# Window attention and a gated feed-forward layer on one core: the whole order of the work written anew, with 363 operations on other engines

## Chip, cores and metric

One of the eight cores of a Trainium2 chip runs one program. The metric is device time in microseconds (us), of which less is better: the median of three runs. A profiled execution of the same program gives the rows below.

## What is computed

```python
# q, k, v: 8 batches x 8 heads x 576 tokens x 64, float32
scores = q @ k.T / sqrt(64)
mask   = (0 <= i - j) & (i - j < 64)              # causal window of 64 tokens
attn   = softmax(where(mask, scores, -1e9))
x      = (attn @ v)                               # as 4608 tokens x 512
h      = x @ w_in                                 # 512 x 2048
g      = h * erf(softplus(h))
out    = g @ w_out                                # 2048 x 512
```

## The kernel before

The 4608 tokens are 36 **units** u of 128 tokens, two units make a **chunk** c of 256, and each chunk has two **groups** g (g = 2c and 2c + 1), one for each half of the 2048 hidden columns. Every float32 operand is split into two float16 parts, high and low, and a product is the sum of three float16 products.

What each instruction does is in some sixty small functions (handlers) at the lines 374 to 805. In which order they are issued is in one string, PLAN, at the lines 52 to 245: 2,696 tokens such as `E:16:0:v`, each a handler's name, its numbers, and often the engine (v VectorE, a ScalarE, g GpSimd). The loop that reads it is the kernel's last:

```python
with tc.manual_schedule(engines=CORE | {ET.SP}):
    for tok in PLAN.split():
        name, *args = tok.split(":")
        HANDLERS[name](*(int(a) if a.isdigit() else a for a in args))
```

Each engine carries out its own instructions in the order of the tokens, and so does SyncE's queue with the DMAs; an instruction waits on semaphores for what it needs. So PLAN decides two things: behind which work on its engine an operation stands, and on which engine it runs.

The stations of the work, by the tokens that this text names:

- **Loads** (SyncE): `lq lk lv` a unit's q, k, v (520 KB for v); `L` one of 16 loads of 1 MB of weights. Weights are split into their parts early (`c d o b h l`, lines 586 to 644).
- **Attention** of unit u: `s` scores (TensorE, line 437), `m` mask and row maximum (VectorE, 454), `f` subtract it (460), `e` two exponentials of a half unit (ScalarE, 474), `r` the low part (482), `t` a transpose by DMA (486), `a` times v (TensorE, 489), `n` normalize (500).
- **Input of the layer**: `xh xl xt`, `T yh yl yt` (529 to 564) split x, form sums of its blocks (`T`, line 545) and turn them by DMA.
- **First matrix product** for groups from 8 on: seven products `M:g:1` to `M:g:7` (line 737; 24 matmuls of 128 columns each) of block sums, after Strassen's scheme. Products 1, 6, 7, 4 are added up in PSUM bank 0, products 2 and 5, 3 in bank 1. Between them `E:g:0` to `E:g:3` (take, line 754) copy bank 0 out, and `C:g:0` to `C:g:2` (join, line 757) add bank 1 to what was copied. The next product into a bank has to wait for the copy before it.
- **Gate**: `sp` softplus and `er` erf (ScalarE, 764 and 768), `gt` (VectorE, 771), `gh gl` the two parts of the result (775, 782).
- **Second matrix product**: `mA` 8 matmuls and `mB` 4 matmuls of 512 columns (line 786), two of each per half group and output bank. `fo` (result, line 795) scales one of the two output banks `o` into `ob`; only then may the next chunk's `mA` write into that bank. `st` stores.

```python
def take(g, k, eng):                                                   # E
    narrow(eng, corner(g, *((0, 0), (0, 1), (1, 1), (1, 0))[k]), bank_view(0))
def result(g, j, eng="v"):                                             # fo
    c, hf = ORDER[g]
    o, co, dst = ops[j], st_g[g], ob[c % 2 if c < 2 else 0][:, j, :]
    if hf == 0 or joint(g):
        scaled(eng, dst, o, co)
```

`e`, `sp` and `er` each need a function table of ScalarE that the other two don't use; where the order goes from one to another, a table load stands ahead. Copies and scalings on ScalarE need none. `narrow` and `scaled` are the helpers at lines 513 and 363, so a row of `E` on ScalarE stands at L515, on VectorE at L517, one of `fo` at L365 or L367; `C` stands at L759, `M` at L745, `mA` and `mB` at L791.

In PLAN the tokens of the last four chunks repeat from chunk to chunk almost word for word; those ahead of them repeat nowhere.

Of the kernel before, what the change touches and what calls it, by code (L numbers as in the profile page):

```python
# [19 lines left out]
W = 64  # L20
# [32 lines left out]
    "lq:0 lv:0 lk:0 lm L:0 lv:1 s:0 pk:0:2:v c:0 m:0:1 m:0:0 f:0:1:g L:1 lq:1 f:0:0:v pk:1:2:v tp:0:1 d:0 e:0:1 pa:0 "  # L53
    "o:0 tp:0:0 pb:0 e:0:0 px:0 d:1 c:1 o:1 py:0 lk:1 L:8 b:0:a pc:0 b:1:a L:3 s:1 a:0:0 L:9 m:1:1 L:2 c:8 d:8 m:1:0 "
    "f:1:0:g lq:2 a:0:1 mb:0 lk:2 o:8 mx:0 my:0 mc:0 c:3 h:0:a n:0 h:1:a d:3 f:1:1:g tp:1:0 e:1:0 tp:1:1 c:9 d:9 "
    "e:1:1 xp:0 c:2 xh:0:a l:0 L:11 o:3 s:2 o:9 d:2 o:2 m:2:1 f:2:1:g b:8:a m:2:0 b:3:a L:10 a:1:0 xl:0 c:11 a:1:1 "
    "b:9:a tp:2:1 b:2:a f:2:0:g tp:2:0 n:1 mb:1 e:2:1 l:1 lq:3 xp:1 d:11 lk:3 lv:2 c:10 xh:1:a L:4 mx:1 e:2:0 o:11 "
    "b:11:a lq:4 lv:3 my:1 mm:0:0:0 d:10 s:3 mc:1 lk:4 xl:1 mb:4 h:3:a a:2:1 c:4 o:10 d:4 l:3 m:3:1 o:4 m:3:0 "
    "pk:3:2:v mm:0:0:1 mm:0:1:1 a:2:0 h:2:a f:3:1:g pk:2:2:v pk:4:0:a L:5 mm:0:1:0 b:10:a b:4:a tp:3:1 mx:4 my:4 "
    "lk:5 pa:1 pb:1 f:3:0:g lq:5 l:2 px:1 c:5 d:5 py:1 L:7 mb:5 pk:5:1:a e:3:1 pc:1 dc:0:g ev:0:1:a d:7 n:2 ev:0:0:a "  # L60
    "o:5 L:6 lv:4 c:7 tp:3:0 pk:4:1:a e:3:0 U:0:7:0:0:g pk:5:0:a xh:2:a a:3:1 a:3:0 U:0:7:1:0:v o:7 pk:4:2:v "
    "mm:0:2:1 mc:4 mm:0:2:0 d:6 mm:0:3:0 n:3 mx:5 my:5 W:0 b:5:a mc:5 mb:2 lv:5 pk:5:2:v U:0:7:2:0:g pa:2 mx:2 c:6 "
    "xl:2:g xh:3:v pb:2 xt:3:0 xl:3:v b:7:a ev:0:2:a sp:0:0 h:8:a px:2 xt:3:1 h:9:g my:2 mm:0:3:1 py:2 er:0:0 h:10:a "
    "xt:2:0 V:0 l:8 o:6 pc:2 mm:1:0:1 qh:5:v mc:2 ev:0:3:a xt:2:1 mm:1:1:1 kh:5:a gt:0:0 b:6:a l:10 l:9 dc:1:g mb:3 "
    "h:4:a mm:1:1:0 mm:1:0:0 qh:4:v vh:5:a kh:4:g h:5:a ev:1:1:a kl:4 ql:4 mm:1:3:1 h:11:a kl:5 ev:1:0:a l:5 lk:7 "
    "sp:0:1 mm:1:3:0 mm:1:2:0 s:4 l:4 l:11 ql:5 vl:5 lq:6 L:12 mm:1:2:1 gh:0:0:a Uh:0:7:0:a m:4:0 vh:4:a mA:0:0:1 "
    "mx:3 gn:0:v mA:0:0:0 m:4:1 vl:4 my:3 ev:1:3:v sp:1:0 er:0:1 ev:1:2:a mc:3 h:6:v Ul:0:7:0:g er:1:0 s:5 gt:0:1 "
    "L:13 mm:2:0 h:7:a dc:2:v c:12 d:12 mm:2:1 gl:0:0 o:12 lv:7 c:13 lk:6 pk:7:1:a mB:0:0:0 l:7 d:13 pk:6:0:a "
    "pk:6:1:a ev:2:0:a mB:0:0:1 lv:6 l:6 f:4:0:g gh:0:1:a o:13 e:4:0 mm:2:2 ev:2:1:a U:1:7:0:0:v f:4:1:g lq:7 "
    "pk:7:0:a mA:0:1:1 gl:0:1 pk:7:2:v pk:6:2:v pa:3 U:1:7:1:0:v pb:3 r:4:0:g e:4:1 px:3 mm:2:3 m:5:0 f:5:0:v py:3 "  # L70
    "r:4:1:v U:1:7:2:0:g pc:3 b:13:a b:12:a m:5:1 t:4:0 qh:7:g dc:4:g t:4:1 mA:0:1:0 mb:6 mB:0:1:1 e:5:0 gt:1:0 mx:6 "
    "f:5:1:v my:6 ev:2:3:v ev:2:2:a mm:3:0 mc:6 kh:6:a e:5:1 h:13:v a:4:0 r:5:1:v dc:3:v a:4:1 gh:1:0:v mB:0:1:0 "
    "ql:7 h:12:a mm:3:1 n:4 r:5:0:g ev:3:0:a sp:2:0 t:5:0 l:12 fo:0:1:a mm:3:2 vh:6:g lq:9 fo:0:0:a l:13 t:5:1 "
    "sp:1:1 kh:7:a L:14 a:5:0 L:15 a:5:1 kl:6 qh:6:v ql:6 vl:6 s:6 ev:3:1:a kl:7 mm:3:3 m:6:1 sp:2:1 vh:7:g d:14 "
    "er:1:1 er:2:0 xh:4:a f:6:1:g n:5 e:6:1 xh:5:a gl:1:0 mA:1:0:1 mB:1:0:1 m:6:0 dc:5:g lv:8 xl:4:g mA:1:0:0 gt:1:1 "
    "f:6:0:g c:15 ev:3:3:v xl:5:v d:15 xt:4:0 gh:1:1:a lq:8 c:14 lk:8 gl:1:1 e:6:0 mB:1:0:0 ev:3:2:a xt:4:1 o:14 "
# [12 lines left out]
    "xt:7:1 ev:5:3:a a:8:0 xt:7:0 e:9:0 pb:5 px:5 mm:5:2 ev:5:2:a py:5 U:1:5:0:2:v gt:4:1 U:3:7:2:0:g U:0:5:0:1:v "
    "mA:4:0:0 U:1:5:1:2:v U:0:5:1:1:v xt:6:1 mA:4:0:1 n:8 mm:6:1 pc:5 r:9:0:v dc:6:g dc:7:v e:9:1 U:0:5:2:1:v mm:6:0 "  # L90
    "gh:4:1:a vh:10:a r:9:1:v xh:8:v gt:5:0 t:9:0 qh:10:a ev:6:1:a kh:10:a gl:4:1 mm:6:3 gl:4:0 kl:10 mB:4:0:1 "
    "xt:8:0 Uh:0:5:1:a U:1:5:2:2:g t:9:1 Uh:1:5:2:a ev:6:0:a Ul:0:5:1:v ql:10 kh:11:a lq:12 ev:6:3:a Ul:1:5:2:v "
    "kl:11 vl:10 qh:11:a s:10 st:0:1 Uh:3:7:0:v a:9:1 m:10:0 ql:11 sp:5:1 a:9:0 mA:4:1:1 vh:11:g U:0:6:0:1:v st:0:0 "
    "lk:12 vl:11 m:10:1 n:9 f:10:1:v mB:4:0:0 U:1:6:0:2:v mm:7:1 sp:6:0 U:1:6:1:2:v er:5:1 s:11 mB:4:1:1 U:0:6:1:1:g "
    "gh:5:0:a lv:12 er:6:0 Uh:0:6:1:a mm:6:2 lk:13 pk:12:0:a Ul:0:6:1:v mA:5:0:1 mA:4:1:0 lv:13 mB:4:1:0 U:2:5:0:1:v "
    "f:10:0:g lq:13 Ul:3:7:0:v ev:7:1:a pk:12:1:a pk:13:0:a m:11:0 pk:13:1:a pk:13:2:v e:10:0 pk:12:2:v pa:6 gt:5:1 "
    "pb:6 gt:6:0 U:2:5:1:1:g U:2:5:2:1:g gl:5:0 Uh:1:6:2:v gh:5:1:a mA:5:0:0 Uh:2:5:1:a ev:6:2:a mB:5:0:0 e:10:1 "
    "Ul:2:5:1:v Ul:1:6:2:v mB:5:0:1 sp:6:1 r:10:0:v gh:6:0:a mm:7:0 dc:11:g m:11:1 px:6 U:3:5:0:2:v py:6 gl:5:1 "
    "U:2:6:0:1:v pc:6 ev:7:0:a U:2:6:1:1:v mm:7:3 r:10:1:g U:3:5:1:2:v f:11:1:v U:0:3:0:0:v mA:5:1:1 sp:7:0 kh:12:a "
    "U:0:3:1:0:v kh:13:a mA:5:1:0 mB:5:1:0 er:6:1 gn:5:v U:3:5:2:2:v xl:8:v kl:12 er:7:0 mB:5:1:1 kl:13 fo:5:0:a "  # L100
# [772 lines left out]
```

## Time and profile before

| | |
|---|---|
| median of 3 runs | 874.83 us (871.86 to 876.56) |
| the profiled execution, its own time | 875.01 us |
| its span in the trace | 873.2 us |
| TensorE busy | 821.2 us, 94% |
| VectorE, ScalarE, GpSimd busy | 725.9, 690.2, 230.2 us |
| mean granted TensorE clock | 0.988 |

TensorE is busy in nearly all of the span, VectorE and ScalarE in four fifths of it, though more at the beginning than at the end. A busy share alone does not say who waits for whom: that is in the waits, the timeline and the stretches.

### The profile page before, as it was taken

The numbers are of one execution on the slowest core, as the hardware profiler recorded it, in microseconds if no ns is written. First come the engines' busy times: TensorE is split into PE (matmuls) and PEld (weight loads), VectorE is DVE, ScalarE is ACT, GpSimd is POOL, SyncE is SP. The second block draws the span as 40 slices with busy tenths as digits, with TensorE's granted clock in tenths as the row PEclk, the third lists the DMA queues.
The fourth block names the chain that finished last, engine by engine and source line by source line (L and its number), as shares of the span: only waits on it lengthen the run. The fifth ranks groups of instructions, "written<-read, shape, count | busy, mean of one in ns | idle before, by whom it ended". The sixth has DMA issues, their size and how long they took to land.

```text
span 873.2 us, 25365 instructions
## 1 busy us (share of the span) xinstructions
PE 821.2 (94%) x10868; PEld 588.2 (67%) x10868; DVE 725.9 (83%) x1610; ACT 690.2 (79%) x823; POOL 230.2 (26%) x206
## 2 busy tenths in 40 slices
PE   3879999999999999998999999999999999999988
PEld 3768666576677677686666767666776767676743
DVE  5999999999999889997989798779999886545351
ACT  4999899989998988787877897477889788465541
POOL 2142352522163342233231334132102322010000
PEclk9889999999999999999999999999999999999999
DMA  9955282751584366374364736543746232220000
GB/s 357 403 169 213 49 228 60 147 153 43 86 192 114 100 166 123 98 132 123 80 143 94 143 81 128 109 109 59 168 74 167 52 74 54 45 56 2 26 25 25
DMA packets 152321, 101.92 MB, mean 117 GB/s; under 512 B 129552, under 2 KB 129680, under 8 KB 152208
## 3 DMA queue, kind: packets, MB, share of 16 engines
q1 hardware_dynamic: 152208, 100.30, 46.6%
q8 instruction: 85, 1.39, 0.7%
q14 instruction: 28, 0.23, 0.1%
HBM read 59.64 MB, written 9.44 MB: 79 GB/s over the span
## 4 chain that ended last, share of the span: by engine, by line
PE 43%; DVE 18%; ACT 10%; DMA 5%; issue 3%; SPq 1%; POOL 0%; DVEq 0%; ACTq 0%; POOLq 0%
PE o L791 22%; PE hp L745 19%; DVE y L773 2%; ACT y L765 2%; DMA pt<-p 2%; DVE vs L372 2%; DVE gl L372 2%; PE av L497 1%; DVE sm L457 1%; ACT L765 1%; DVE ks L372 1%; DVE h L759 1%; DMA vr<-v_in 1%; PE s L448 1%; DVE arena L729 1%
## 5 line engine op out<-in xcount | busy, mean ns | idle before, releaser
L791 PE MATMUL o<-w,gh 128*128 128x512 f16 x1152 | 270.2, 381 | 4.8 <-ACT ob L365 4.5
L791 PEld LDWEIGHTS <-gh 128*128 128x128 f16 x1152 | 109.3, 98 | 123.8 <-issue 7.1
L745 PEld LDWEIGHTS <-w 128*128 128x128 f16 x2688 | 157.1, 98 | 20.6 <-issue 4.0
L745 PE MATMUL hp<-arena,w 128*128 128x128 f16 x2688 | 166.3, 220 | 3.3 <-ACT h L515 1.9
L791 PE MATMUL o<-w,gl 128*128 128x512 f16 x576 | 144.5, 379 | 0.0
L745 PE MATMUL hp<-arena 128*128 128x128 f16 x2016 | 127.2, 220 | 8.2 <-DVE h L517 4.5
L745 PEld LDWEIGHTS <-arena 128*128 128x128 f16 x2016 | 118.9, 98 | 23.1 <-issue 10.7
L773 DVE TENSOR_TENSOR y<-h,y 128x1024 f32<-128x1024 f32 x72 | 90.6, 1264 | 27.2 <-ACT y L769 27.2
L765 ACT ACT_TABLE_LOAD x46 | 59.0, 1283 | 49.2 <-DVE h L759 47.2
L515 ACT ACTIVATE h<-hp 128x512 f32<-128x512 f32 x101 | 59.1, 586 | 48.5 <-PE hp L745 37.9
L701 PE MATMUL hp<-arena,w 128*128 128x256 f16 (+1 forms) x960 | 90.7, 254 | 4.7 <-DMA arena<-arena 2.2
L759 DVE TENSOR_TENSOR h<-hp,h 128x512 f32<-128x512 f32 x84 | 57.5, 685 | 43.5 <-PE hp L745 42.9
L372 DVE SCALAR_TENSOR_TENSOR gl<-y,sgc,gh 128x1024 f16<-128x1024 f32 x64 | 85.5, 1340 | 7.2 <-PE o L791 7.2
L701 PEld LDWEIGHTS <-w 128*128 128x128 f16 x960 | 78.6, 99 | 16.1 <-issue 4.4
L765 ACT ACTIVATE y<-h,c 128x1024 f32<-128x1024 f32 x72 | 81.7, 1145 | 7.6 <-DVE h L759 7.0
L791 PEld LDWEIGHTS <-gl 128*128 128x128 f16 x576 | 52.6, 98 | 50.6 <-DVE gl L372 0.2
L462 POOL TENSOR_TENSOR sm<-sm,mx 128x512 f32<-128x512 f32 x43 | 55.8, 1300 | 97.9 <-DVE mx L457 78.2
L769 ACT ACTIVATE y<-y 128x1024 f32<-128x1024 f32 x72 | 74.7, 1053 | 0.5
L484 POOL TENSOR_TENSOR p<-sm,p 128x512 f16<-128x512 f32 x31 | 43.8, 1415 | 114.7 <-ACT sm L480 105.6
L457 DVE CUSTOM_DVE_ANT_0 sm<-s,mask 128x128 f32<-128x128 f32 x288 | 65.5, 283 | 3.4 <-PE s L448 2.7
L769 ACT ACT_TABLE_LOAD x47 | 60.3, 1283 | 0.8
L480 ACT ACTIVATE sm<-sm,shift,cde 128x512 f32<-128x512 f32 x64 | 52.1, 814 | 2.1
(169 smaller groups left out, 1169.6 us busy)
## 6 DMA issues: line engine op xcount, KB each, us to landing
vr<-v_in SPq DMA_DIRECT2D x36, 520.0 KB, 4.5
kr<-k_in SPq DMA_DIRECT2D x36, 384.0 KB, 4.8
qr<-q_in SPq DMA_DIRECT2D x36, 256.0 KB, 3.7
out<-ob SPq DMA_DIRECT2D x34, 256.0 KB, 2.5
arena<-w_in SPq DMA_DIRECT2D x4, 1024.0 KB, 9.5
w<-w_in SPq DMA_DIRECT2D x4, 1024.0 KB, 9.8
arena<-w_out SPq DMA_DIRECT2D x4, 1024.0 KB, 6.6
w<-w_out SPq DMA_DIRECT2D x2, 1024.0 KB, 14.3
```

The costliest lines, as they stand in the source:

```text
L372: nc.vector.scalar_tensor_tensor(dst, src, s, hi, op0=ALU.mult, op1=ALU.subtract)
L457: nc.vector.tensor_tensor_reduce(smi(u, par)[:, j, :], sps[par][:, j, :], mask[:, var, :], 1.0, LOWEST, op0=ALU.add, op1=ALU.max, accum_ou ...
L462: eng_of(eng).tensor_tensor(s, s, m.unsqueeze(2).broadcast_to([P, HP, P]), op=ALU.subtract)
L480: nc.scalar.activation(s, s, AF.Exp, bias=shift14, scale=es)
L515: nc.scalar.activation(dst, src, AF.Copy)
L701: nc.tensor.matmul(hps[pc % 2][:, f, at_t], w1[a][hf][:, cc, fs], xt[b][c % 2][:, cc:2 * NCC:NCC, :][:, at_x, :], start=(n == 0), stop=(n ...
L745: nc.tensor.matmul(bank[:, q, f, :], left(m, a, 2 * hf + q)[:, cc, f * P:(f + 1) * P], xt[b][c % 2][:, slot + cc, :], start=m in (1, 2, 5) ...
L759: nc.vector.tensor_tensor(dst, bank_view(1), dst, op=ALU.add)
L765: nc.scalar.activation(at(yb, g, n), at(hb, g, n), AF.Softplus, scale=st_c[g][:, n:n + 1])
L769: nc.scalar.activation(y, y, AF.Erf)
L773: nc.vector.tensor_tensor(y, at(hb, g, n), y, op=ALU.mult)
L791: nc.tensor.matmul(ops[j], a[:, f // 2, j, f % 2, :], w2[b][:, hf * GF + f, :], start=f == 0 and a is gh and b == 0 and not (joint(g) and hf),
```

## The change

PLAN is another string of the same 2,696 operations; nothing else in the file differs, except that PLAN has one line more, so that every line number behind it is higher by one. Announced was "a new pattern of two units repeated from chunk 6 on, joined to the beginning; some on other engines". The string shows no such pattern: from one chunk to the next, or to the next but one, hardly half of any engine's tokens stand in the same order, in the last chunks too. The order differs from the first token on.

Of the 2,696 operations 363 run on another engine than before; most of these moves cancel. What is left, by the counts of the tokens: `fo` from 28 on ScalarE and 12 on VectorE to 19 and 21; `T` from 18 on GpSimd and 24 on VectorE to 24 and 18; `f` from 43 on GpSimd and 29 on VectorE to 46 and 26; `E` from 74 on ScalarE and 38 on VectorE to 72 and 40; `gn` from 7 on GpSimd to 12; and one to three each of `h qh kh vh xh xl yh yl pk ev gh r U Ul`. In sum ScalarE has 16 of these operations fewer (573 to 557), VectorE 5 fewer (920 to 915), GpSimd 21 more (188 to 209).

```diff
 PLAN = (
...
-    "pk:22:2:v M:16:1 gt:14:0 C:15:2 f:20:1:g lq:23 lk:23 gh:13:1:v yt:8:1:1 gt:14:1 E:16:0:v M:16:6 f:20:0:g "
...
-    "mA:33:0:0 gl:33:1 mB:33:0:1 er:34:1 M:35:4 mB:33:0:0 M:35:3 gh:34:0:v mA:33:1:1 E:35:3:v C:35:2 sp:35:0 "
-    "mA:33:1:0 gt:34:1 st:15:0 er:35:0 mB:33:1:1 gl:34:0 sp:35:1 fo:33:1:a st:16:1 mB:33:1:0 gh:34:1:v mA:34:0:1 "
...
+    "xh:18:v gt:14:1 mB:13:0:0 mA:13:1:0 pk:22:1:a gh:14:0:a st:5:1 M:15:3 pk:22:0:a M:16:1 s:21 yt:8:1:0 pk:23:2:v "
+    "pa:11 T:9:0:v e:20:1 pb:11 C:15:2 mB:13:1:1 m:21:0 f:21:0:g E:16:0:v yt:8:0:1 M:16:2 gh:14:1:a m:21:1 px:11 "
+    "fo:13:1:a mB:13:1:0 t:20:0 py:11 yt:8:1:1 pc:11 dc:18:v M:16:6 gl:14:0 mA:14:0:1 yh:9:0:a E:16:1:v xl:18:v "
...
+    "M:35:5 er:34:0 mB:33:1:0 C:35:1 M:35:4 st:15:1 M:35:3 fo:33:0:a gt:34:0 E:35:3:v gh:34:0:a gh:34:1:v gl:34:0 "
+    "st:16:0 mB:33:1:1 mA:34:0:0 C:35:2 fo:33:1:v mB:34:0:0 sp:35:0 mA:34:0:1 gl:34:1 er:35:0 mB:34:0:1 mA:34:1:0 "
...
```

ScalarE's order near the end of the program, before: from the erf of group 34 to the second erf of group 35 (h0 and y0 hold groups of even number, h1 and y1 those of odd number; hp0 is PSUM bank 0; o0 and o1 are the output banks). `L765` is softplus, `L769` erf; `ob<-o1` and `ob<-o0` are `fo:33`.

```order
L769 ACTIVATE y0_137<-y0_137 128x1024 x2
L765 ACT_TABLE_LOAD
L765 ACTIVATE y1_138<-h1_136,c1_87 128x1024
L769 ACT_TABLE_LOAD
L769 ACTIVATE y1_138<-y1_138 128x1024
L765 ACT_TABLE_LOAD
L765 ACTIVATE y1_138<-h1_136,c1_87 128x1024
L365 ACTIVATE ob_141<-o1_148,sg_88 128x512
L365 ACTIVATE ob_141<-o0_147,sg_88 128x512
L769 ACT_TABLE_LOAD
L769 ACTIVATE y1_138<-y1_138 128x1024
```

The same place in the changed order, up to the last scaling, `fo:35`:

```order
L770 ACTIVATE y0_137<-y0_137 128x1024
L366 ACTIVATE ob_141<-o0_147,sg_88 128x512
L366 ACTIVATE gh_139<-y0_137,sgc_90 128x1024
L766 ACT_TABLE_LOAD
L766 ACTIVATE y1_138<-h1_136,c1_87 128x1024
L770 ACT_TABLE_LOAD
L770 ACTIVATE y1_138<-y1_138 128x1024
L766 ACT_TABLE_LOAD
L766 ACTIVATE y1_138<-h1_136,c1_87 128x1024
L770 ACT_TABLE_LOAD
L770 ACTIVATE y1_138<-y1_138 128x1024
L366 ACTIVATE ob_141<-o1_148,sg_88 128x512
```

Before, both scalings of chunk 16's result (`fo:33`) stand behind three table loads and the first three of group 35's four softplus and erf operations. Now one of the two stands ahead of them, and the other is on VectorE.

ScalarE's order where the products of group 32 begin, before: `h0<-hp0` is `E:32:0`.

```order
L769 ACT_TABLE_LOAD
L769 ACTIVATE y0_137<-y0_137 128x1024 x2
L765 ACT_TABLE_LOAD
L765 ACTIVATE y1_138<-h1_136,c1_87 128x1024
L769 ACT_TABLE_LOAD
L769 ACTIVATE y1_138<-y1_138 128x1024
L515 ACTIVATE h0_135<-hp0_145 128x2x256
L765 ACT_TABLE_LOAD
L765 ACTIVATE y1_138<-h1_136,c1_87 128x1024
```

And in the changed order (`h1<-hp0` is `E:31:3`; `h0<-hp0` are `E:32:0`, and then `E:32:1` and `E:32:2`):

```order
L766 ACT_TABLE_LOAD
L766 ACTIVATE y0_137<-h0_135,c1_87 128x1024
L516 ACTIVATE h1_136<-hp0_145 128x2x256
L770 ACT_TABLE_LOAD
L770 ACTIVATE y0_137<-y0_137 128x1024
L516 ACTIVATE h0_135<-hp0_145 128x2x256
L366 ACTIVATE ob_141<-o0_147,sg_88 128x512
L766 ACT_TABLE_LOAD
L766 ACTIVATE y1_138<-h1_136,c1_87 128x1024
L516 ACTIVATE h0_135<-hp0_145 128x2x256 x2
```

Here three copies out of bank 0 stand each right behind an operation that loads a table, where before it was one. In the whole order ScalarE loads a table 138 times, before 129 times: for `e` 35 (32), for `sp` 49 (46), for `er` 50 (47), and 4 others.

## Rows read from the trace of the kernel before

**Rows 1.** Five stretches: busy us (instructions) by engine, clock granted, DMA share, GB/s.

```profile
0.00:100.00 100.00, 75.15 (x988) 63.02 (x989) 87.54 (x236) 83.77 (x112) 26.74 (x38) 0.93 0.68 252
100.00:275.00 175.00, 169.74 (x2136) 116.81 (x2137) 170.34 (x409) 165.72 (x208) 67.07 (x54) 1.00 0.56 130
275.00:600.00 325.00, 311.36 (x4508) 226.11 (x4504) 286.59 (x640) 260.16 (x309) 102.72 (x86) 0.99 0.51 112
600.00:825.00 225.00, 224.00 (x3001) 161.48 (x2999) 163.76 (x313) 163.41 (x179) 33.64 (x30) 1.00 0.35 73
825.00:873.20 48.20, 40.94 (x254) 20.81 (x250) 17.66 (x18) 17.10 (x17) 0.00 (x0) 0.95 0.06 23
```

**Rows 2.** TensorE timeline, the end: start, us, line, matmuls, [idle before <-releaser].

```profile
838.02 3.62 PE L791 MATMUL o<-w,gh 128*128 128x512 f16 x16
841.48 1.89 PE L791 MATMUL o<-w,gl 128*128 128x512 f16 x8
846.88 5.30 PE L791 MATMUL o<-w,gh 128*128 128x512 f16 x16 [3.51 <-ACT ob L365]
```

**Rows 3.** Timeline of ScalarE in the same stretch.

```profile
843.81 1.28 ACT L765 ACT_TABLE_LOAD   x1
845.11 1.15 ACT L765 ACTIVATE y<-h,c 128x1024 f32<-128x1024 f32 x1
846.16 1.24 ACT L365 ACTIVATE ob<-o,sg 128x512 f32<-128x512 f32 x2
```

**Rows 4.** A stretch of 5 us at the end, columns as in rows 1.

```profile
845.00:850.00 5.00, 3.12 (x11) 1.26 (x11) 0.19 (x1) 4.73 (x6) 0.00 (x0) 0.81 0.28 105
```

**Rows 5.** Waits of TensorE, whole run: us in total, times, longest us.

```profile
PE hp L745 <- ACT h L515: 5.0, 6, 2.1
PE s L469 <- POOL sm L462: 4.9, 3, 2.2
PE o L791 <- ACT ob L365: 4.5, 2, 3.5
PE hp L745 <- DVE h L517: 4.5, 2, 2.7
```

**Rows 6.** Timeline of TensorE, waits of the middle and of the last third.

```profile
396.69 1.50 PE L745 MATMUL hp<-arena,w 128*128 128x128 f16 x24
400.86 2.90 PE L745 MATMUL hp<-arena 128*128 128x128 f16 x24 [2.67 <-DVE h L517]
...
423.36 1.89 PE L791 MATMUL o<-w,gh 128*128 128x512 f16 x8 [1.01 <-ACT ob L365]
...
570.13 1.50 PE L745 MATMUL hp<-arena 128*128 128x128 f16 x24 [2.07 <-ACT h L515]
...
804.20 1.50 PE L745 MATMUL hp<-arena 128*128 128x128 f16 x24 [0.50 <-ACT h L515]
```

**Rows 7.** Timeline of ScalarE ahead of 570.13 us.

```profile
567.16 1.28 ACT L765 ACT_TABLE_LOAD   x1 [6.10 <-DVE h L759]
568.45 1.15 ACT L765 ACTIVATE y<-h,c 128x1024 f32<-128x1024 f32 x1
569.51 0.58 ACT L515 ACTIVATE h<-hp 128x512 f32<-128x512 f32 x1
```

**Rows 8.** Groups by line and shape: xcount | busy us, mean ns | idle before.

```profile
L773 DVE TENSOR_TENSOR y<-h,y 128x1024 f32<-128x1024 f32 x72 | 90.6, 1264 | 27.2 <-ACT y L769 27.2
...
L765 ACT ACT_TABLE_LOAD x46 | 59.0, 1283 | 49.2 <-DVE h L759 47.2 <-DVE den L505 1.3
...
L462 POOL TENSOR_TENSOR sm<-sm,mx 128x512 f32<-128x512 f32 x43 | 55.8, 1300 | 97.9 <-DVE mx L457 78.2 <-DVE den L505 8.2 <-DMA arena<-arena 6.0
...
L462 DVE TENSOR_TENSOR sm<-sm,mx 128x512 f32<-128x512 f32 x29 | 20.7, 720 | 0.2
...
L365 ACT ACTIVATE ob<-o,sg 128x512 f32<-128x512 f32 x26 | 17.4, 676 | 22.5 <-PE o L791 17.4 <-DMA out<-ob 5.0
...
L367 DVE TENSOR_SCALAR ob<-o,sg 128x512 f32<-128x512 f32 x8 | 5.8, 741 | 0.0
```

379 rows, old and new, of the table PLAN are left out of this document.

## Prediction, made before the changed kernel was run

> **What bounds the kernel now.** I read the stretches first, then TensorE's waits, then its timeline at the waits that matter. In the stretches [rows 1] the reader is to see where TensorE is not busy. In the first 100 us that is 100 - 75.2 = 24.8 us; there VectorE and ScalarE work 88 and 84 of 100 us, and GpSimd stands in TensorE's way too (4.9 us) [rows 5]. From 100 to 275 us it is 5.3 us, with VectorE and ScalarE busy 97% and 95%. From 275 to 600 us it is 13.6 us, though VectorE has room (287 of 325 us). From 600 to 825 us it is 1.0 us: this part, where the order repeats from chunk to chunk, is as good as TensorE allows. In the last 48.2 us it is 7.3 us. The order takes no matmul away and moves none to another engine, so the 821 us that TensorE is busy are the floor, and the change can only win or lose in these gaps, 52 us in all.
>
> Who ends the gaps of the middle stands in the waits [rows 5]: the copy of bank 0 by ScalarE (5.0 us in 6 waits) and by VectorE (4.5 us in 2), and the scaling of a result by ScalarE (4.5 us in 2, of which 3.5 us at the very end). The DMAs hardly show after the first loads.
>
> A gap can cost more than itself. After the wait of 2.67 us at 398 us, 24 matmuls take 2.90 us where the same 24 take 1.50 us elsewhere [rows 6]; after the 3.51 us at the end, 16 take 5.30 us instead of 3.62 us [rows 2], and the granted clock of that stretch is 0.81 of the 2.4 GHz level, a mean of that level and the lower one [rows 4]. So I count these two waits with 1.40 and 1.68 us on top, and give shorter ones no surcharge: after those of 1.01, 2.07 and 0.50 us the matmuls take their usual time [rows 6].
>
> **The end: -5.2 us.** Before, the two scalings of chunk 16 stand on ScalarE behind three table loads and three of group 35's operations. TensorE has the bank's last matmul done at 841.48 + 1.89 = 843.4 us [rows 2], but ScalarE begins the scaling only at 846.16 us, after the load at 843.81 us and the softplus at 845.11 us [rows 3]. The loss is 3.51 + 1.68 = 5.19 us. In the new order one scaling stands ahead of these loads and the other on VectorE, directly behind the last join; the end then hangs on group 35's chain. From the last product's end TensorE has 4 + 48 matmuls left ahead of group 35, and 16 of them take 841.48 - 838.02 = 3.46 us [rows 2], so 52 take 11.2 us. The chain before took from 838.02 to 843.81 us, 5.8 us, up to the end of the first erf [rows 2, 3]; the gate (1.26 us [rows 8]) and the high part, a VectorE operation that I put no longer than the gate, make it 8.3 us. The join now stands behind one more low part, for which I allow another 1.3 us: 9.6 us, against 11.2 us of cover. So I take the whole 5.2 us; the bounds are 0 (the chain is late by another cause) and 5.2.
>
> **Results elsewhere: -1.0 us.** The only other wait for a scaling is 1.01 us at 423 us [rows 6]. In the old order three of 30 scalings outside the beginning had 1.4 us or less of matmuls between the last into their bank and the next; in the new one none has less than 2.6 us. Bounds 0 and -1.0. For it nine more scalings run on VectorE (0.74 us each, 6.7 us) and nine fewer on ScalarE (0.68 us each) [rows 8].
>
> **Product 6 of group 16: -2.0 us.** In the old order this product follows product 1 directly, in the same bank, and TensorE waits 2.67 us for the copy and loses 1.40 us after it: 4.07 us [rows 6]. In the new order scores, product 2 and eight matmuls lie between, 4.0 us. But the turned sums that this product reads (`yt:8:1:1`) stand just ahead of it in both orders, and may have been the later condition. Bounds 0 and -4.1; I take the middle.
>
> **Copies behind table loads: +3.1 us.** The order adds nine table loads, from 129 to 138, of 1.28 us each [rows 8], 11.5 us on ScalarE. As load it is covered: 16 operations leave ScalarE (the nine scalings alone are 6.1 us), and from 275 us on, where the loads are added, it is idle for 65 + 62 + 31 us [rows 1]. What costs is the place. ScalarE takes its work in order, so a copy of bank 0 that stands behind a softplus or an exponential with a load waits for both. The rows ahead of 570.13 us show it: load 1.28, softplus 1.06 to the next row, copy 0.58, and TensorE waits 2.07 us for it [rows 7, 6]. I counted along both orders the copies on ScalarE that stand right behind an operation with a load and have less than 2.6 us of matmuls between the two products: 8 before, 13 now. All waits for such copies came to 5.0 us [rows 5], so at most 5.0 / 8 = 0.62 us a place, and five more places cost 3.1 us. Bounds: 0, and five times the 2.07 us of the worst, 10.4.
>
> The Trainium skill, "ScalarE: Activation LUTs", section "What ACT_TABLE_LOAD costs", puts a switch at about 2.66 us, load and drain. In this trace the operation behind a load starts 1.28 to 1.30 us after the load starts, and no such drain shows [rows 3, 7]. By the page's figure the nine loads would be an estimated 23.9 us of ScalarE instead of 11.5.
>
> **The beginning and the moves to GpSimd: 0.** The first three loads are the same, in another order; the first weight load now stands behind a second load of v (0.52 MB; at the 252 GB/s of the first stretch [rows 1] 2.1 us at most, beside other loads). The bounds are +2.1 us and -4.9 us, the latter if GpSimd's shift no longer holds TensorE up [rows 5]. I take 0, as both orders do the same work up to there. GpSimd gets 21 operations more. A shift is 1.30 us there and 0.72 on VectorE [rows 8], so some 21 x 1.3 = 27 us, beside an engine that idles three quarters of the time. They free VectorE of about as much as the scalings add to it, so its load is level.
>
> **Sum.** 875.0 (the profiled execution's own time, 1.8 us over its span) - 5.2 - 1.0 - 2.0 + 3.1 = 869.9 us, taken as **870.0**. The median of the three runs is 874.83, 0.2 us lower; the sum stands for either.
>
> **Rivals.** (1) *Slower by copies behind loads.* If each of the 13 places costs the 2.07 us of the worst row, they cost 26.9 instead of 5.0 us: 875.0 - 6.2 + 21.9 = 890.7 us; the point from which it decides is 0.9 us a place, where it has eaten the 6.2 us of end and results. For it: the last third, clean before, now has four of these places with only 0.86 us of matmuls as cover, and the loads are nine more. Against it: two of the old ones with the same cover cost 0.50 us at most (804.20 us [rows 6]), as ScalarE was done by then. The Trainium skill's same page, section "Table sets: the hidden batching unit", advises to batch by set, and would count these loads against the new order too. Chance 0.22; I expect some 885 rather than 891. (2) *Given back.* The last third loses at the rate of the middle, 13.6 / 325 us, in 225 us: 9.4 instead of 1.0 us. With the end and the results won and the other terms nil that is 875.0 - 6.2 + 8.4 = 877.2 us, no difference. For it: the repeating order is gone, and no part of the new one is like it. Chance 0.18. (3) *Better throughout.* The middle reaches the rate of the last third, 1.0 / 225 us: 1.4 instead of 13.6 us, and 875.0 - 5.2 - 12.2 = 857.6 us. For it: the shortest covers are gone (none is zero). Against it: 5 covers of under 0.9 us remain in bank 0, where there were 6. Chance 0.15. (4) *The announced pattern* isn't there, so nothing repeats a gain or a stall from chunk to chunk; that keeps all of this small, and has no time of its own.
>
> **Numbers.** The forecast has 0.45. A difference of 0.5%, 4.4 us, is about what a measurement of this kernel can tell from no change, and 870.0 lies just beyond it, so I give 0.28 of the forecast to faster and 0.17 to same. Faster: 0.28 + 0.15 = 0.43. Same: 0.17 + 0.13 (most of 2) = 0.30. Slower: 0.22 + 0.05 = 0.27. The forecast's own terms reach from 875.0 - 5.2 - 1.0 - 4.1 - 4.9 = 859.8 to 875.0 + 10.4 + 2.1 = 887.5 us with every bound bad; the range of 857 to 886 takes in rival 3 and most of rival 1.
>
> **What would show it.** End: no wait of TensorE for `ob` above 1 us in the last 40 us, a granted clock of 1.00 there, the last product's end followed by some 22 us of matmuls. Copies: TensorE's waits for ScalarE's copies at 8 us, not 5. Group 16: no wait above 1 us ahead of its product 6. Last third: TensorE idle under 3 us in the 225 us before the end's stretch. Wrong would be a wait that is not in [rows 5] at all, such as one for a transpose, or a first 100 us of work that takes longer by over 3 us.

## The result, and the profile after

The changed kernel takes 860.23 us (median of 4 runs, 859.62 to 861.30); the kernel before, beside it, 874.42 us (4 runs, 871.86 to 876.56). The ratio is 0.984, with a 95% interval of 0.981 to 0.987: faster, by 11 to 17 us. The profiled execution took 861.3 us, its span is 859.5 us (873.2 before), and the granted clock 0.986 over the whole span. Line numbers are one higher than in the rows of before, and two or three higher in the experiments further down.

The same stretches as in [rows 1], with the last one of equal length:

```profile
0.00:100.00 100.00, 75.66 (x982) 63.46 (x983) 86.53 (x240) 82.33 (x109) 32.07 (x43) 0.91 0.73 251
100.00:275.00 175.00, 168.70 (x2091) 116.96 (x2090) 166.66 (x385) 165.07 (x216) 67.49 (x52) 0.99 0.55 126
275.00:600.00 325.00, 319.75 (x4651) 231.82 (x4649) 297.18 (x660) 278.06 (x316) 116.93 (x96) 0.99 0.54 116
600.00:811.30 211.30, 211.18 (x2822) 150.93 (x2821) 156.29 (x303) 148.95 (x163) 49.09 (x38) 1.00 0.35 76
811.30:859.50 48.20, 44.32 (x330) 25.02 (x328) 19.25 (x20) 19.08 (x19) 0.00 (x0) 1.00 0.06 23
```

Read the first column of busy time, TensorE, against the length of the stretch. It idles 24.3, 6.3, 5.3, 0.1 and 3.9 us, where it idled 24.9, 5.3, 13.6, 1.0 and 7.3 us. The sum is 39.9 us instead of 52.0, so 12.1 us less idle; the busy time fell by another 1.6 us (from 821.2 to 819.6 us). Together that is the 13.7 us by which the span is shorter. Nearly all of it is in the middle (8.4 us) and at the end (3.4 us). The stretches are cut at equal times, not at equal work, so a little of it can stand on either side of a cut. GpSimd is busy 35.4 us longer in all (265.6 instead of 230.2 us).

The waits of TensorE over the whole run, as [rows 5]: total, times, longest:

```profile
PE av L404 <- DVE cmx L358: 5.7, 3, 2.7
PE s L470 <- POOL sm L463: 4.6, 4, 2.2
PE hp L702 <- ACT h L516: 3.7, 1, 3.7
PE av L615 <- DVE arena L508: 3.5, 1, 3.5
...
PE hp L746 <- ACT h L516: 1.0, 2, 0.6
...
PE o L792 <- ACT ob L366: 0.5, 1, 0.5
PE hp L746 <- DVE h L518: 0.4, 1, 0.4
```

The three entries for which the prediction had terms have nearly gone: copies by ScalarE 5.0 to 1.0 us, copies by VectorE 4.5 to 0.4, results 4.5 to 0.5. The wait for GpSimd is what it was. Another entry leads now, behind the 6.7 us for the first load: the product over a chunk's peaks (`pb`, L404) waits for VectorE's maximum, 5.7 us, where it had waited 1.2 us. The 3.7 us (at the first matrix product of the groups below 8, L702) and the 3.5 us are in the first 100 us.

TensorE's timeline at the end, as [rows 2]:

```profile
839.92 3.62 PE L792 MATMUL o<-w,gh 128*128 128x512 f16 x16
843.37 1.89 PE L792 MATMUL o<-w,gl 128*128 128x512 f16 x8
845.10 3.62 PE L792 MATMUL o<-w,gh 128*128 128x512 f16 x16
```

and ScalarE's ahead of it, as [rows 3]:

```profile
831.40 0.69 ACT L366 ACTIVATE ob<-o,sg 128x512 f32<-128x512 f32 x1 [4.98 <-PE o L792]
832.46 1.15 ACT L366 ACTIVATE gh<-y,sgc 128x1024 f16<-128x1024 f32 x1 [0.38 <-DVE y L774]
833.63 1.28 ACT L766 ACT_TABLE_LOAD   x1
835.92 1.15 ACT L766 ACTIVATE y<-h,c 128x1024 f32<-128x1024 f32 x1 [1.01 <-DVE h L760]
```

The one scaling of chunk 16 that is left on ScalarE (831.40 us) now stands ahead of the three table loads, the other is on VectorE, and no row of TensorE has an idle time in front of it. Sixteen matmuls take 3.62 us throughout, none takes the 5.30 us of before.

Table loads ahead of softplus, as [rows 8]:

```profile
L766 ACT ACT_TABLE_LOAD x49 | 62.9, 1283 | 34.9 <-DVE h L760 28.8 <-DVE gl L373 4.6 <-DVE w L373 0.9
...
```

Loads ahead of softplus went from 46 to 49 (those ahead of the exponentials from 32 to 35, of erf from 47 to 50), at the same 1.28 us each. So the changed kernel pays for nine more loads, and yet TensorE waits less for ScalarE behind the first 100 us (2.0 us in all instead of 9.8). Within them it waits more (8.5 instead of 1.6 us), and there it idles as long as before.

### The profile page after: what moved, and what is told of

It reads as the page before. It is cut to its first block, busy times and chain, and to the rows that moved or that the text cites. A ratio compares the mean times of both kernels' runs of the same rounds, so it can differ in the third digit from the quotient of the medians.

```text
span 859.5 us, 25374 instructions
## 1 busy us (share of the span) xinstructions
PE 819.6 (95%) x10868; PEld 588.2 (68%) x10868; DVE 725.9 (84%) x1605; ACT 693.5 (81%) x819; POOL 265.6 (31%) x227
## 4 chain that ended last, share of the span: by engine, by line
PE 56%; DVE 13%; ACT 5%; DMA 3%; issue 2%; POOL 1%; SPq 0%; DVEq 0%; POOLq 0%; ACTq 0%
PE o L792 29%; PE hp L746 23%; PE av L498 2%; DMA vr<-v_in 2%; PE s L449 2%; DVE y L774 1%; DVE gl L373 1%; DVE sm L458 1%; DVE vs L373 1%; DMA arena<-arena 1%; DVE ks L373 1%; DVE arena L730 1%; ACT y L766 1%; ACT L766 1%; DVE qs L373 1%
## 5 line engine op out<-in xcount | busy, mean ns | idle before, releaser
L746 PEld LDWEIGHTS <-w 128*128 128x128 f16 x2688 | 157.6, 98 | 18.1 <-issue 1.8
L746 PE MATMUL hp<-arena 128*128 128x128 f16 x2016 | 124.7, 219 | 2.7 <-DMA arena<-arena 1.3
L746 PEld LDWEIGHTS <-arena 128*128 128x128 f16 x2016 | 117.0, 98 | 14.1 <-issue 3.5
L774 DVE TENSOR_TENSOR y<-h,y 128x1024 f32<-128x1024 f32 x72 | 88.6, 1236 | 19.0 <-ACT y L770 18.9
L702 PE MATMUL hp<-arena,w 128*128 128x256 f16 (+1 forms) x960 | 94.6, 261 | 3.7 <-ACT h L516 3.7
L516 ACT ACTIVATE h<-hp 128x512 f32<-128x512 f32 x97 | 56.7, 586 | 48.7 <-PE hp L746 40.2
L702 PEld LDWEIGHTS <-w 128*128 128x128 f16 x960 | 81.6, 102 | 15.2 <-issue 4.3
L463 POOL TENSOR_TENSOR sm<-sm,mx 128x512 f32<-128x512 f32 x46 | 61.3, 1336 | 98.5 <-DVE mx L458 98.1
L485 POOL TENSOR_TENSOR p<-sm,p 128x512 f16<-128x512 f32 x34 | 46.7, 1380 | 105.9 <-ACT sm L481 87.4
```

What stands on the lines that cost most here:

```text
L463: eng_of(eng).tensor_tensor(s, s, m.unsqueeze(2).broadcast_to([P, HP, P]), op=ALU.subtract)
L516: nc.scalar.activation(dst, src, AF.Copy)
L702: nc.tensor.matmul(hps[pc % 2][:, f, at_t], w1[a][hf][:, cc, fs], xt[b][c % 2][:, cc:2 * NCC:NCC, :][:, at_x, :], start=(n == 0), stop=(n ...
L746: nc.tensor.matmul(bank[:, q, f, :], left(m, a, 2 * hf + q)[:, cc, f * P:(f + 1) * P], xt[b][c % 2][:, slot + cc, :], start=m in (1, 2, 5) ...
L774: nc.vector.tensor_tensor(y, at(hb, g, n), y, op=ALU.mult)
```

## The experiments

All times are medians; each ratio is to the kernel before as it ran beside the experiment on the same chip.

### Where in time the gain lies: two kernels joined at group 16

In `old_then_new`, the tokens of before stand up to the first product of group 16 (1,391 of 2,696), then what is left in the changed order; each token has the engine of its own kernel. `new_then_old` is the reverse.

The joint of the first, against before:

```diff
-M:16:1 gt:14:0 C:15:2 f:20:1:g lq:23 lk:23
+M:16:1 s:21 pk:23:2:v pa:11 e:20:1 pb:11
...
```

and of the second, against the changed kernel:

```diff
-M:16:1 s:21 yt:8:1:0 pk:23:2:v pa:11 T:9:0:v
+M:16:1 C:15:2 yt:8:1:1 E:16:0:v M:16:6 e:20:1
...
```

> The order and engines of before up to the first product of group 16, and from there on what is left in the changed kernel's order and on its engines. Theory A by stretches: the idle time that went lies in groups 16 to 22 (8 to 9 us) and at the end (5 us), both behind the joint, so this has the whole gain: 859 to 864 us. Rival D, the new pattern repeated from chunk 6 (group 12) on is what pays, all along: at most two thirds of the gain, 865 us or more. Rival E, the new beginning buys the rest's gain: 870 us or more.

> The order and engines of the changed kernel up to the first product of group 16, and from there on those of before. Theory A by stretches: the stretch ahead of group 16 gave nothing (TensorE idles 30.6 us in the first 275 us of the changed kernel, 30.1 before): 872 to 877 us. Rival D: a third of the gain or more is here, 870 us or less. Rival E: 865 us or less. In all of these the joint itself can cost a wait of 1 to 4 us.

Measured: `old_then_new` 861.89 us, ratio 0.987 (0.986 to 0.989); `new_then_old` 877.22 us, ratio 1.005 (1.003 to 1.006). The second half of the order has 11 us of the 14 by itself. The first half alone, with a joint, is 4 us slower than before, 0.2 us above what theory A expected of it; its waits for the copies of `hp` and for results are as long as ever (waits of TensorE, whole run):

```profile
PE hp L748 <- ACT h L518: 6.2, 7, 1.9
...
PE o L794 <- ACT ob L368: 4.0, 2, 3.5
```

Rival D (the new pattern from chunk 6 on pays all along) and rival E (the beginning) fall. The remaining 0.3% between 0.987 and 0.984 is within what the two intervals leave open.

### Where in the second half: the joint at group 22

The same with the joint at the first product of group 22.

```diff
-M:22:1 pk:28:1:a sp:21:0 E:22:0:v yt:11:1:1 sp:21:1
+M:22:1 mB:19:1:1 pk:29:2:v sp:21:1 E:22:0:a pa:14
...
```

> The kernel before up to the first product of group 22, from there on what is left in the changed kernel's order and on its engines. With the joint at group 16 the time was 861.9 us. Theory by stretches: in the kernel before TensorE waited 8.0 us between groups 16 and 21 for copies, joins and a result (2.67, 0.67, 1.01, 0.64, 0.85, 0.36 and 1.80 us), and those stay, while the 3.3 us of groups 22 to 24 and the 3 to 5 us of the end go: 866 to 869 us. Rival, the end and the last third are all that matters: 861 to 863 us. Rival, the middle is all: 871 to 875 us.

Measured: 864.99 us, ratio 0.989 (0.988 to 0.991), that is, 1 us below the lower end of what was expected of the theory by stretches and 2 us above that of the first rival. The waits of groups 16 to 21 are still there in TensorE's timeline, while from 600 us on it has none:

```profile
401.59 0.22 PE L747 MATMUL hp<-arena 128*128 128x128 f16 x1 [2.67 <-DVE h L519]
...
414.45 1.50 PE L747 MATMUL hp<-arena,w 128*128 128x128 f16 x24 [1.88 <-ACT h L517]
...
424.17 1.89 PE L793 MATMUL o<-w,gh 128*128 128x512 f16 x8 [1.01 <-ACT ob L367]
```

What lies behind group 22 is worth some 9 us. The kernel joined at group 16 is about 2 us faster than this one (0.987 against 0.989, and the intervals overlap), though groups 16 to 21 show 8 us of waits. Not all of these 8 us were there to be won. In `tail_alone` (next), whose order is the same up to there, the same waits come to 6.0 us; and in `old_then_new` they are gone, but one of 2.08 us for the peaks has come.

### The end alone

Against before:

```diff
-fo:33:1:a
+fo:33:1:v
...
-fo:33:0:a
+fo:33:0:v
```

> The kernel before with one edit: the two scalings of group 33's results (fo:33:1 and fo:33:0) on VectorE instead of ScalarE, where they stood behind table loads. By the prediction's term for the end: 5.2 us less, 866 to 870 us beside 873 to 875 of the kernel before, ratio 0.994, and no wait of TensorE for ob over 1 us. Rival, the wait goes over to the gating chain of the last groups (sp, er, gt, gh of 34 and 35): under 2 us less, ratio 0.998 to 1.000, and a wait for gh or gl in its place.

Measured: 868.89 us, ratio 0.994 (0.993 to 0.996), 4.6 us less. TensorE's timeline at the end:

```profile
841.88 3.61 PE L793 MATMUL o<-w,gh 128*128 128x512 f16 x16
```

and the same stretch of 5 us as in [rows 4]:

```profile
845.00:850.00 5.00, 5.00 (x25) 2.25 (x23) 2.36 (x2) 2.50 (x3) 0.00 (x0) 1.00 0.00 0
```

Both the idle time and the slow matmuls behind it are gone, at a clock of 1.00 instead of 0.81. Two tokens' engines bring a third of the gain; the gating chain (`sp`, `er`, `gt`, `gh`) did not become the bound.

### Group 16 alone

Against before, `M:16:2` moved ahead by some tokens:

```diff
+M:16:2
 M:16:6 f:20:0:g
...
-M:16:2
```

> The kernel before with one move: the second product of group 16 (M:16:2, bank 1) put between the first and the sixth (both bank 0), so that TensorE has work while VectorE copies bank 0. By the prediction's term: the wait of 2.67 us, and the matmuls behind it that ran slowly, go: 2.0 us less (bounds 0 and 4.1), ratio 0.9953 to 1.000. Rival, the wait only moves to the next product whose copy VectorE holds: no difference, and a wait over 1 us elsewhere in group 16.

Measured: 873.39 us, ratio 1.000 (0.998 to 1.001): no difference. TensorE's timeline in group 16:

```profile
401.99 1.50 PE L747 MATMUL hp<-arena 128*128 128x128 f16 x24 [1.33 <-DVE h L519]
...
414.06 1.50 PE L747 MATMUL hp<-arena,w 128*128 128x128 f16 x24 [2.67 <-ACT h L517]
```

ScalarE's, ahead of the second of these waits:

```profile
408.13 1.28 ACT L767 ACT_TABLE_LOAD   x1
409.43 1.15 ACT L767 ACTIVATE y<-h,c 128x1024 f32<-128x1024 f32 x1
410.60 1.28 ACT L771 ACT_TABLE_LOAD   x1
411.89 1.06 ACT L771 ACTIVATE y<-y 128x1024 f32<-128x1024 f32 x1
412.85 0.67 ACT L367 ACTIVATE ob<-o,sg 128x512 f32<-128x512 f32 x1
413.42 0.59 ACT L517 ACTIVATE h<-hp 128x512 f32<-128x512 f32 x1
```

The same copy on ScalarE in the kernel before, and the operation with which the work ahead of it began:

```profile
400.78 0.84 ACT L391 ACTIVATE junk<-kr 128x768 uint8<-128x768 f32 x1 [4.45 <-DMA kr<-k_in]
...
413.00 0.59 ACT L515 ACTIVATE h<-hp 128x512 f32<-128x512 f32 x1
```

and the product on TensorE that waited for it there:

```profile
413.63 1.50 PE L745 MATMUL hp<-arena,w 128*128 128x128 f16 x24 [0.67 <-ACT h L515]
```

The wait of 2.67 us behind product 1 became 1.33 us, and the 24 matmuls behind it take their 1.50 us. But TensorE arrives earlier at product 4, and that one waits for the copy `E:16:2`, which stands on ScalarE behind softplus and erf of group 15, each with a load, and a result. ScalarE reaches that copy at 413.4 us, as it did before (413.0). Waits and slow matmuls of the group came to 2.67 + 1.40 + 0.67 = 4.7 us before and to 1.33 + 0.27 + 2.67 = 4.3 us now (the 0.27 us is a wait at product 7). ScalarE's queue set when the group ended, and the wait at product 6 stood inside its slack. That queue was late from further up: until 400.78 us ScalarE had stood idle for 4.45 us, waiting for the load of k whose largest value `pk:23:1` takes, and from there it worked without a pause up to the copy.

In the changed order the copy on ScalarE waits for TensorE:

```profile
414.90 0.60 ACT L516 ACTIVATE h<-hp 128x512 f32<-128x512 f32 x1 [0.21 <-PE hp L746]
```

There the copy before it (`E:16:1`) is on VectorE, 3.0 us of matmuls instead of 1.7 lie between products 7 and 4, and no wait of TensorE in group 16 is above 0.25 us. Which of these differences did it was not tried.

### The copies behind table loads

Two of the seven places, against before:

```diff
-sp:24:1 E:25:0:a
+E:25:0:a sp:24:1
...
-er:33:0 mB:31:1:1 gl:32:0 E:34:0:a
+E:34:0:a er:33:0 mB:31:1:1 gl:32:0
```

> The kernel before with seven of its eight copies of bank 0 that stood behind an operation with a table load moved ahead of it (E:9:0 ahead of e:13:0, E:18:2 of e:23:0, E:25:0 of sp:24:1, E:28:0, E:30:0, E:32:0 and E:34:0 of er of the group before). By the prediction's term for these places, at up to 0.62 us each: 2 to 4.3 us less, ratio 0.995 to 0.998. Rival, such a place costs nothing where enough products stand between, and the copies that were waited for were late for another reason: within 1 us, ratio 0.999 to 1.001.

Measured: 879.53 us, ratio 1.005 (1.003 to 1.007), 6 us more, which neither side had expected. ScalarE's timeline around `sp:24:1` and `E:25:0`, in the kernel before:

```profile
613.01 1.28 ACT L765 ACT_TABLE_LOAD   x1
614.30 1.15 ACT L765 ACTIVATE y<-h,c 128x1024 f32<-128x1024 f32 x1
615.36 0.58 ACT L515 ACTIVATE h<-hp 128x512 f32<-128x512 f32 x1
...
624.73 0.58 ACT L515 ACTIVATE h<-hp 128x512 f32<-128x512 f32 x1
```

in the experiment, where two softplus follow each other (the row of 2.19 us), from the moved copy down to the next one:

```profile
615.08 0.60 ACT L517 ACTIVATE h<-hp 128x512 f32<-128x512 f32 x1 [1.90 <-DVE y L775]
615.70 1.28 ACT L767 ACT_TABLE_LOAD   x1
616.99 2.19 ACT L767 ACTIVATE y<-h,c 128x1024 f32<-128x1024 f32 x2
...
626.93 0.57 ACT L517 ACTIVATE h<-hp 128x512 f32<-128x512 f32 x1
```

and TensorE's timeline in the experiment, at the product behind that copy, and the longest of its waits from there to the last 40 us:

```profile
627.55 2.84 PE L747 MATMUL hp<-arena,w 128*128 128x128 f16 x48 [2.08 <-ACT h L517]
...
772.27 1.89 PE L793 MATMUL o<-w,gh 128*128 128x512 f16 x8 [1.06 <-ACT ob L367]
```

In before, ScalarE did the load and the softplus while TensorE worked at the product whose copy came next: the copy stood behind a load and cost nothing. With the copy ahead, ScalarE stands idle for 1.90 us first. The trace puts that down to VectorE's gate of group 23, which reads the buffer that the copy writes and ends about when the product does. So the copy comes only 0.28 us earlier (615.08 for 615.36), but the load starts 2.7 us later (615.70 for 613.01), all that follows is later, and the copy `E:25:2` ends at 627.5 instead of 625.3 us. TensorE waits 2.08 us for it, in a stretch where it had waited for nothing. So here the copy was well placed behind the load: the load ran while the copy's input was still being made. This is one of the places. In the last third the two waits of 0.50 us for copies are gone, and three for results have come, 1.55 us in sum. The profiled execution, at 876.5 us the shortest of the five, doesn't show all of the 6 us.

### Order and engines apart

One kernel has the changed order with all 363 operations back on their old engines; the other the old order with the new engines.

A few of the tokens of the first, in the changed order, against the changed kernel:

```diff
-pk:27:1:a
+pk:27:1:v
...
-dc:23:v
+dc:23:g
...
-E:20:1:v
+E:20:1:a
```

and of the second, in the old order, against before:

```diff
-pk:27:1:a
+pk:27:1:v
...
-yh:11:1:a
+yh:11:1:v
...
-fo:17:0:a
+fo:17:0:v
```

> The changed kernel's order, with each operation on the engine that it had before (363 tokens set back). Theory A, the places: the gain comes from where copies, scalings and joins stand between TensorE's products, and which engine does one hardly matters: 859 to 864 us, ratio to the kernel before 0.983 to 0.988, and TensorE's waits for copies of hp stay at about the 1.4 us of the changed kernel. Theory B, the engines: the gain comes from the 35 us that go from VectorE and ScalarE to GpSimd: 870 us or more. Rival C: order and engines were made for each other, and either alone is worse than the kernel before: above 876 us.

> The order of the kernel before, with each operation on the engine that the changed kernel gives it. Theory A, the places: no gain beyond the results of the end (group 33's scalings are on VectorE here, so up to 5 us): 869 to 876 us, and the copies of hp are waited for 4 us or more on each engine, as before. Theory B, the engines: 860 to 864 us. Rival C, made for each other: above 876 us, since copies now stand on the other engine at places chosen for the first one.

Measured: 943.24 us, ratio 1.081 (1.079 to 1.084), and 942.71 us, ratio 1.080 (1.078 to 1.082). Theories A and B both fall; C holds, far beyond its bound: either half of the change costs 70 us, both together save 14. The waits of TensorE in the first of them, whole run:

```profile
PE hp L747 <- ACT h L517: 16.1, 10, 3.9
PE av L405 <- DVE cmx L359: 13.5, 6, 2.9
PE o L793 <- ACT gh L367: 7.3, 4, 2.1
```

and one of its stretches, columns as in [rows 1]:

```profile
100.00:275.00 175.00, 152.98 (x1684) 101.95 (x1682) 155.02 (x334) 141.41 (x177) 56.05 (x39) 0.94 0.44 106
```

The loss isn't in one place: most kinds of waits grew. And no engine is busy all the time. In that stretch VectorE and ScalarE, which are busy 167 and 165 of 175 us in the changed kernel, are busy 155 and 141 us: they idle more too.

### Which of the 363: two families set back

Against the changed kernel, two of the 50 tokens of the first:

```diff
-E:20:1:v
+E:20:1:a
...
-E:28:1:a
+E:28:1:v
```

and three of the 185 of the second, which came to GpSimd or left it:

```diff
-r:24:0:g
+r:24:0:v
...
-dc:23:v
+dc:23:g
...
-qh:27:g
+qh:27:a
```

> The changed kernel with one family set back: the 50 copies of bank 0 that changed between ScalarE and VectorE (26 to VectorE, 24 to ScalarE) are on their old engine, at the changed kernel's places. Setting all 363 operations back cost 83 us. Theory C1: these copies carry it, since TensorE's next product of bank 0 waits for each (ten waits for ScalarE's copies, 16.1 us, were the largest entry there): 890 us or more. Theory C2: the mismatch is spread over all families, by their number (50 of 363): about 872 us (860 + 83 x 50/363 = 871.6), between 864 and 885.

> The changed kernel with only the operations set back that came to GpSimd or left it (subtractions of the row maximum, remainders of exponentials, sums for the products, scale products and some scalings): GpSimd then holds what it held before, 35 us less at the changed kernel's places. Theory B': the relief of the other engines by GpSimd is what makes the changed order possible: 890 us or more. Theory C2, spread by number: these are about 180 of 363, so about half of the 83 us, 895 to 905 us. Theory C1, the copies of bank 0 alone decide: 875 us or less.

Measured: 880.49 us, ratio 1.009 (1.006 to 1.012), and 891.43 us, ratio 1.021 (1.018 to 1.023). Beside the changed kernel's 860.2 us that is 20 us for 50 copies and 31 us for 185 operations, while all 363 cost 83 us. C1 (the copies decide) falls: they carry a quarter. C2 (spread by number) has the first in its range, but its 872 us was 8.5 us too low, and its 895 to 905 us for the second too high: a copy of bank 0 weighs more than its share (0.4 us each, against 0.17 for one of the 185). B' expected 890 us or more of the second, and got it, but so much would also come of a plain mismatch; whether GpSimd's 35 us of extra work pay as relief stays open. What TensorE waits for most (whole run) is copies in the first:

```profile
PE hp L747 <- ACT h L517: 11.2, 10, 4.3
```

and the peaks in the second:

```profile
PE av L405 <- DVE cmx L359: 11.3, 7, 2.8
```

### Two mended versions

The largest waits that the changed kernel has left were taken away by moves: `pb` of chunks 5 and 13 one product later, and in the second version also five operations of the first 100 us.

One of the two places, against the changed kernel:

```diff
-pb:13 gt:18:1 px:13 mA:17:1:0 M:20:1 T:11:2:g M:19:3 E:20:0:v st:7:0 py:13 C:19:2 dc:23:v M:20:6 pc:13
+gt:18:1 mA:17:1:0 M:20:1 pb:13 T:11:2:g M:19:3 E:20:0:v px:13 st:7:0 C:19:2 dc:23:v M:20:6 py:13 pc:13
```

and the first of the moves that the second version adds:

```diff
+mx:4 n:2
 o:10
...
-mx:4
...
-n:2
```

> The changed kernel with the two largest waits left behind its first 100 us taken away: the products over the peaks of chunks 5 and 13 (pb, with px, py and pc behind them) come one TensorE product later, so that VectorE has the peaks ready. The waits were 2.67 and 2.55 us, and the 24 matmuls behind each took 4.44 us for 2.78 and 2.52 for 1.50. If the wait costs what it shows and nothing else is late there: 3 to 7.9 us less than the changed kernel, 852 to 857 us, ratio 0.975 to 0.981. Rival, the next operation was held up by another engine just as long: within 1.5 us of the changed kernel, 859 to 862 us.

> As the one before, and in the first 100 us: the row maximum's normalisation n:2 and the weight maximum mx:4 ahead of o:10 on VectorE, mb:5 behind a:3:1 on TensorE, the copies ev:0:0 ahead of b:10 and ev:0:3 ahead of er:0:0 on ScalarE. TensorE waits there 3.49 us for VectorE and 3.65 us for ScalarE's ev:0:3 behind a table load. If both waits go and the rest keeps its pace: up to 7 us less than the one before, 847 to 853 us. Rival, the first 100 us are set by ScalarE and by the loads (TensorE idles 24 us there), so the wait moves to the next operation: no gain, 853 to 860 us.

Measured: 861.23 us (6 runs, 857.4 to 864.5), ratio 0.986 (0.984 to 0.989), and 858.83 us (6 runs, 855.9 to 865.2), ratio 0.985 (0.981 to 0.988). Neither can be told from the changed kernel. Waits of TensorE in the first one, whole run; that for the peaks is smaller (2.0 for 5.7 us), that for ScalarE's copies in the groups below 8 larger (5.6 for 3.7 us):

```profile
PE hp L703 <- ACT h L517: 5.6, 2, 3.7
...
PE av L405 <- DVE cmx L359: 2.0, 3, 1.5
```

One of the new waits stands in its timeline at 173.7 us, where the changed kernel had waited 2.67 us for the peaks and now ScalarE is late:

```profile
173.73 2.78 PE L703 MATMUL hp<-arena,w 128*128 128x256 f16 x24 [1.91 <-ACT h L517]
```

So the rival of each has the better of it: a wait that was mended gave way to the next. In the second version the two waits at the beginning fell from 3.7 to 0.3 and from 3.5 to 0.7 us, and TensorE still idles 24.1 us in the first 100 us (24.3 in the changed kernel). No version tried is faster than the changed kernel by more than the noise.

## Why the prediction was right in its sign and too small in its size

The forecast was 870.0 us, a gain of 4.9; measured were 860.2 us, a gain of 14. The range (857 to 886) holds it; faster was the likeliest sign. Of the cases, rival 3 ("better throughout", 857.6 us, given a chance of 0.15) came nearest: it had the middle's 13.6 us of idle fall to 1.4, and it fell to 5.3.

- **The end, -5.2 us: right.** Alone it gives -4.6 us (by the ratio's interval, 0.9928 to 0.9958 of 873.5 us, 3.7 to 6.3 us). Both the 3.51 us and the longer matmuls went, at a clock of 1.00; the surcharge for those matmuls is that of one execution, though (last section). Group 35's chain had the cover that was worked out for it: 7.5 us from the end of the last product to the first high part (9.6 forecast), beside 11.1 us of matmuls.
- **Results elsewhere, -1.0 us: right as a wait.** That of 1.01 us at 423 us is gone, and one of 0.53 us at 227 us has come; its worth was not tried by itself.
- **Product 6 of group 16, -2.0 us: wrong as a step of its own.** The wait went, as forecast, but taken away alone it is worth 0.1 us (ratio 0.998 to 1.001). The step failed at "loses 1.40 us after it: 4.07 us": it priced the wait by its length, without asking what was late next. ScalarE's queue was, by 2.67 us, two products of bank 0 further on.
- **Copies behind table loads, +3.1 us: wrong, and the main term that made the forecast too small.** The step that failed is "at most 5.0 / 8 = 0.62 us a place, and five more places cost 3.1 us". The count was right, the nine more loads are there, and TensorE's waits for these copies fell from 5.0 to 1.0 us. The price of a place isn't in what stands ahead of the copy, but in whether the product that feeds it ends before that work does. In the kernel before, seven copies moved ahead of such work made it 6 us slower, and the place followed in rows shows why; for the five new places it is argued, not tried. [rows 7] already held a sign of it: the load there starts only after ScalarE's 6.10 us of idle time, when VectorE's join ends, so that the 2.07 us were not the load's alone. The bound of 0 was too high as well, as far as waits tell: those for ScalarE's copies fell by 4.0 us, and those for VectorE's, which had no term but that of group 16, by 4.1. What that is worth in time no run shows by itself, and group 16 shows that it need not be its length.
- **GpSimd and the beginning, 0: right in sum.** The wait for GpSimd is 4.6 us (4.9 before). The 21 operations more are 35.4 us of its time, not 27. The first 100 us idle 24.3 instead of 24.9 us.
- **What had no term: the waits behind group 22.** By the joint there about 9 us of the gain lie behind it, 4.6 of them at the end; some 4 us come from groups 22 to 34, about what the waits there held (2.07 us at 570 us, 1.20 at 592 us, and twice 0.50 us in the last third; all but the 1.20 us are among the copies above). That these waits are the cause is argued from the rows; no run takes them away alone. The prediction looked at group 16's wait alone and priced the others by the mean of its term for copies.

Of what was named as signs, these came out: no wait for `ob` in the last 40 us, clock 1.00 there, no wait in group 16, 0.1 us idle in the stretch from 600 us on (under 3 forecast), and 21.6 us of matmuls behind the last product (some 22 forecast). "Waits for copies at 8 us" came out wrong, in the gain's favour. And one sign of "wrong" did show: a wait that is not in [rows 5], for the peaks, 5.7 us (1.2 us before, not among those rows).

Rival 1 (slower by copies behind loads, 890.7 us) had its condition, five more places and nine more loads, but not its price: four of the places are in the last third, which idles 0.1 us. The Trainium skill, "ScalarE: Activation LUTs", section "Table sets: the hidden batching unit", advises to batch by set; by that rule nine more switches would speak against the new order. As a count the trace doesn't bear it out here, since the 11.5 us lie on an engine that had room. In the small no run decides: in the changed order's group 16 two softplus stand behind one load and the copy behind them is in time, and in the experiment on copies behind table loads two softplus stand behind one load and the next copy is 2.2 us late. Rival 2 (the last third at the middle's rate) falls by the same 0.1 us. Rival 4 named no time, and no run here shows what repetition is worth.

## What to carry to other kernels

Price a wait by what would be late next, on the engine that is next, not by its length: a wait of 2.67 us with slow matmuls behind it was worth nothing by itself, while two scalings at the end, with nothing behind them, gave 4.6 of the 5.2 us that the rows promised. Where each engine takes its work strictly in order, a copy behind slow work is well placed if that work runs while the copy's input is still being made; count places only after laying both timelines side by side. And an order and its choice of engines are one thing: judge them together, since half of a good change can cost five times what the whole of it saves.

## What was not expected of the hardware

That idle time of TensorE costs more than itself was read from two waits of one execution. It isn't so in each. In the profiled execution of the experiment on copies behind table loads, the same two waits stand in TensorE's timeline, and the matmuls behind them take 1.50 and 3.61 us, where they had taken 2.90 and 5.30 us:

```profile
403.05 1.50 PE L747 MATMUL hp<-arena 128*128 128x128 f16 x24 [2.67 <-DVE h L519]
...
850.04 3.61 PE L793 MATMUL o<-w,gh 128*128 128x512 f16 x16 [3.51 <-ACT ob L367]
```

In the 5 us around that last wait the granted clock is 1.00, where it was 0.81. So the 1.40 and 1.68 us that the prediction counted on top belong to its execution; a surcharge is worth counting only as something that can come or stay away.

How far it adds up was not expected either. In the kernel with new order and old engines TensorE is busy 841.2 us with the same matmuls that take 819.6 us in the changed kernel, at a granted clock of 0.97 against 0.986 over the span: 102 us of idle time there, 40 us here, and 22 us more of busy time on top. By the distances between the starts of matmuls that follow each other in the two traces, an estimated 14 us of the 22 are slower matmuls. What the rest is was not tried; more gaps alone lengthen it, since a matmul of 512 columns that stands alone shows 0.38 us, and sixteen in a row 3.62 us.
